# Two transfer cuts in a decode attention + gated MLP kernel: w_up in three transfers, the last wo tile in fewer pieces

## The chip, the core and the metric

The kernel runs on one core of a Trainium2 chip. The metric is the time of one execution in microseconds (us). A core has a matmul engine (PE, with a separate weight-load path, PEld), a vector engine (DVE), a scalar engine (ACT), a general engine (POOL) and a queue engine (SP) that issues most transfers. The transfers themselves are carried by 16 DMA engines, which is what "load engines" means in this text. A transfer is cut into packets, here one packet for one partition's row, and every DMA engine works its packets off in order; after its share of a transfer it sends a small packet of 4 bytes that counts up the transfer's semaphore. A transfer has landed when all its engines have done so.

## What is computed

One decode step for two sequences: y = x + attention(xn) @ wo + (relu(xn @ w_gate) * (xn @ w_up)) @ w_down, where xn is x normalized over its 512 columns. Attention has 32 query heads of 128 over 8 key heads, and looks at the last 4,096 positions of the caches.

```python
q = (xn @ wq) as 32 heads of 128
k, v = the last 4096 positions of k_cache, v_cache (8 heads, each used by 4 query heads)
o = softmax(q k^T / sqrt(128)) v
a = o (2 x 4096) @ wo (4096 x 512)
gate = xn @ W_gate (512 x 1792); gate = gate * (gate > 0)
h = gate * (xn @ W_up)
out = x + a + h @ W_down (1792 x 512)
```

All of it is fp32. The weights and the part of the caches that is used are 94.9 MB, and each byte is read once.

## The kernel before

All loads but x go out from SP, in the order in which the program is written: wq in two transfers, w_gate, w_up, then k and v tiles of 4 MB in turn, w_down, and wo in two tiles. Each of these lands in a tile of a ring of four buffers (tag "ring", 28 or 32 KB in each of the 128 partitions), so that a load can be issued when the tile four places before it has been used. Before the change every load spans 128 partitions; x alone has two rows and goes to partitions 0 and 1.

The middle of the program is a loop over four groups of heads: for each k tile two 32x32 block transposes on DVE (line L253), score matmuls on PE (L258), a softmax, a re-ordering of the weights on DVE (L302), and the matmuls with v (L321).

Names and lines that matter here:

- `load_ff` loads w_gate (tile wg) and w_up (tile wu): 128 partitions with 4 rows of 1,792 floats each, 28 KB in a partition. The matmuls that read them are on L229; first the 16 of w_gate, then the 16 of w_up (u_ps). Their product (L238, L239) is wanted only by the w_down matmuls near the end.
- The last wo tile (r = 1) holds 16 "rows" j of 128 x 512 floats, 2 KB of each partition for one row. It comes in pieces, `cuts` on line L441: rows 0 to 3, 4 to 7, 8 to 11, 12 and 13, 14, each piece with a transfer and a semaphore of its own; row 15 (`last`) follows in two halves of its columns (L449).
- The matmuls at the end take the rows in order. Rows 0 to 7 go the wide way (`project_wide`, L424, tile yw_ps), together with all of the first wo tile; ACT then copies the sum to SBUF (yw, L454). Rows 8 to 14 go the narrow way (`project`, L428, tile y_ps): four matmuls a row, each in two passes. After row 11 the same function folds yw into y_ps. DVE copies y_ps out (yc, L460) when row 14 is in. Row 15 is multiplied last, half by half (z_ps, L464), DVE adds yc to it (yo, L467), and SP sends the result (L469).

The order on each engine is the order of the program text; there is no scheduler. Completion semaphores of the loads are dealt out in turn from a set of eight, so that a load also waits until the load eight places before it has landed.

Of the kernel before, what the change touches and what calls it, by code (L numbers as in the profile page):

```python
# [9 lines left out]
F32 = mybir.dt.float32  # L10
# [10 lines left out]
def kernel(  # L21
# [12 lines left out]
    nc = tc.nc  # L34
    P = 128
# [4 lines left out]
    F = w_gate.shape[1]  # L40
    W = min(4096, max(256, SK // 4))
    KC = D // P
# [17 lines left out]
    ring = ctx.enter_context(tc.tile_pool(name="ring", bufs=RING))  # L60
# [8 lines left out]
    def load(name, src, shape):  # L69
        t = ring.tile(shape, F32, name=name, tag="ring")  # L70
        nc.sync.dma_start(t, src)
        return t
# [5 lines left out]

    def load_ff(w, name):
        return load(name, w.rearrange("(p k) f -> p k f", p=P), [P, KC, F])  # L80

    def load_down():
        return load("wd", w_down.rearrange("(p k) e -> p k e", p=P), [P, FB, D])
# [11 lines left out]
    NJ = HQ * DH // (R * P)  # L95
# [3 lines left out]
    def wo_rows(r, j0, j1):  # L99
        rows = NJ * P  # L100
        return wo[r * rows:(r + 1) * rows, :].rearrange("(p j) e -> p j e", p=P)[:, j0:j1, :]
# [93 lines left out]
    for kc in range(KC):  # L195
        for r in range(R):
            for c in range(C):
# [3 lines left out]
                    start=(kc == 0), stop=(kc == KC - 1),  # L201
                )
    gw = load_ff(w_gate, "wg")
    uw = load_ff(w_up, "wu")
    for r in range(R):
        qs = work.tile([P, 512], F32, name=f"qs{r}", tag="qs")
        (nc.vector.tensor_copy if r else nc.scalar.copy)(qs, q_ps[r])  # L207
# [5 lines left out]
        for m in range(NB):  # L213
            src = qt[32 * m:32 * m + 32, :, :, 0].rearrange("p i (t h) b -> p b t h i", h=2)
            for x in range(Q):
                d = qz[32 * x:32 * x + 32, r * B:r * B + B, m]
                dst = bass.AP(
                    tensor=d.tensor, offset=d.offset + x * TK,
                    ap=[d.ap[0], d.ap[1], [64 + REP, NP], [32, 2], [1, REP]],
# [218 lines left out]
        project_wide(hT[:, k, 0:B], dw[:, k])  # L438
    spread_heads(R - 1)
    wots = []  # L440
    for r, cuts in ((0, (0, NJ)), (1, (0, 4, 8, 12, 14, 15))):  # L441
        wt = ring.tile([P, NJ, D], F32, name=f"wo{r}", tag="ring")
        for j0, j1 in zip(cuts, cuts[1:]):
            nc.sync.dma_start(wt[:, j0:j1], wo_rows(r, j0, j1))
        wots.append(wt)
# [54 lines left out]
```

## Time and profile before

| | |
|---|---|
| median of 3 runs | 228.81 us (228.78 to 228.83) |
| the profiled execution's own time | 228.73 us |
| its span, first to last instruction | 226.9 us |
| granted PE clock, mean | 0.804 |
| busy: PE / DVE / ACT / POOL | 127.3 / 118.6 / 14.1 / 4.3 us |
| bytes moved | 95.03 MB, mean 419 GB/s |

The profiled execution lies 0.08 us under the median of the runs and 0.05 us under the fastest of them. The span leaves out 1.8 us of the execution's own time, which lie before the first and after the last instruction.

How to read it: the profile gives the busy time of each engine, the share of time in which the 16 DMA engines had a packet, and a chain of waits that ends with the last instruction. The view of a stretch of time (a window) gives the same for a part of the span, and the view of the DMA queues for a window gives the number of packets that began in it, their bytes, and the time they took as a share of 16 engines over the window's length. From such a row the mean duration of a packet is share x window x 16 / packets. Queue q1 is SP's, q10 is ACT's (x), q8 carries the instruction fetches.

### The profile page before, as it was taken

How to read it: one execution, taken by the hardware profiler on the slowest of the kernel's cores; microseconds unless marked ns; L12 is line 12 of the kernel's file. 1: busy time of each engine (PE TensorE's matmuls, PEld its weight loads, DVE VectorE, ACT ScalarE, POOL GpSimd, SP SyncE). 2: the span in 40 equal slices, each digit the busy share in tenths (PEclk: the TensorE clock that was granted, in tenths of full speed). 3: DMA queues.
4: the chain of work that ended last, by engine and by line, in shares of the span. 5: the costliest groups of instructions: out<-in, count | busy, mean ns of one | idle time of the engine just before them, and what ended most of it. 6: DMA issues, size and time to landing. Idle time of an engine off the chain costs nothing.

```text
span 226.9 us, 2121 instructions
## 1 busy us (share of the span) xinstructions
PE 127.3 (56%) x888; PEld 37.2 (16%) x888; DVE 118.6 (52%) x159; ACT 14.1 (6%) x41; POOL 4.3 (2%) x15
## 2 busy tenths in 40 slices
PE   0195926502735004885705885936957646869294
PEld 0141211100101001221201211201411201214013
DVE  2400043219893399964599993599369285130001
ACT  2000123000000500000200000200000110000000
POOL 7000000000000000000000000000000000000000
PEclk9999788955796555796985996585997995999589
DMA  7999999998998998998999999999999899999892
GB/s 278 462 393 427 475 414 413 462 445 387 462 456 375 458 456 387 448 462 387 445 462 422 407 462 433 404 456 442 399 450 456 387 448 462 409 423 459 377 414 85
DMA packets 4212, 95.03 MB, mean 419 GB/s; under 512 B 488, under 2 KB 748, under 8 KB 1004
## 3 DMA queue, kind: packets, MB, share of 16 engines
q1 hardware_dynamic: 4196, 94.90, 97.4%
q8 instruction: 7, 0.11, 0.2%
q14 instruction: 1, 0.01, 0.0%
q10 hardware_dynamic: 8, 0.00, 0.0%
HBM read 94.90 MB, written 0.00 MB: 418 GB/s over the span
## 4 chain that ended last, share of the span: by engine, by line
DMA 58%; DVE 23%; PE 12%; issue 3%; ACT 2%; SPq 1%; DVEq 0%; ACTq 0%
DMA k<-in_A_k_cache_dram 38%; DVE kT L253 16%; DMA wo<-in_A_wo_dram 11%; DMA wq<-in_A_wq_dram 9%; DVE pt L302 4%; PE o L321 3%; PE s L258 3%; PE q_ps L199 2%; ACT pz L290 1%; DVE on L330 1%; DVE pT L296 1%; PE y_ps L428 1%; PE oa L341 1%; DVE m L270 1%; ACT L290 1%
## 5 line engine op out<-in xcount | busy, mean ns | idle before, releaser
L253 DVE STREAM_TRANSPOSE kT<-k 128x4096 f32<-128x4096 f32 x16 | 70.6, 4429 | 11.9 <-DMA k<-in_A_k_cache_dram 11.8
L258 PE MATMUL s<-kT,qz 128*32 128x512 f32 x256 | 43.3, 800 | 56.7 <-DVE kT L253 56.7
L321 PE MATMUL o<-v,pt 128*32 128x512 f32 x256 | 33.5, 655 | 0.0
L258 PEld LDWEIGHTS s<-kT,qz 128*32 128x32 f32 x256 | 8.5, 126 | 85.1 <-issue 59.8
L302 DVE COPY pt<-pT 32x256 f32<-32x256 f32 x64 | 18.2, 284 | 1.0
L341 PE MATMUL oa<-on,pick 128*16 128x512 f32 x16 | 10.0, 712 | 6.9 <-DVE on L330 6.9
L221 DVE COPY qz<-qt 32x32 f32<-32x32 f32 x16 | 3.0, 188 | 20.3 <-ACT qz L221 20.3
L199 PE MATMUL q_ps<-wq,xnT 128*32 128x512 f32 x64 | 11.8, 901 | 3.1 <-DMA wq<-in_A_wq_dram 2.7
L321 PEld LDWEIGHTS o<-v,pt 128*32 128x32 f32 x256 | 9.0, 119 | 19.0 <-issue 18.9
L290 ACT ACTIVATE pz<-s,nm 64x512 f32<-64x512 f32 x8 | 5.8, 729 | 80.4 <-DVE nm L284 80.3
L330 DVE TENSOR_TENSOR on<-o,own_u 128x512 f32<-128x512 f32 x8 | 5.4, 672 | 9.9 <-PE o L321 9.8
L460 DVE COPY yc<-y_ps 128x128 f32<-128x128 f32 x1 | 0.3, 292 | 19.4 <-PE y_ps L428 19.4
L296 DVE STREAM_TRANSPOSE pT<-pz 128x1024 f32<-128x1024 f32 x4 | 5.0, 1245 | 8.3 <-ACT pz L290 8.3
L424 PE MATMUL yw_ps<-wo,oT 128*2 128x512 f32 x48 | 6.8, 724 | 4.2 <-DMA wo<-in_A_wo_dram 4.2
L270 DVE TENSOR_REDUCE m<-s 128x1 f32<-128x512 f32 x4 | 2.8, 692 | 11.5 <-PE s L258 11.5
L184 PE MATMUL xt_ps<-rep,xc 2*128 2x32 f32 x8 | 2.1, 419 | 10.7 <-DVE rep L182 10.7
L229 PE MATMUL u_ps<-wu,xnT 128*32 128x448 f32 x32 | 3.2, 542 | 2.8 <-DMA wu<-in_B_W_up_dram 2.8
L199 PEld LDWEIGHTS q_ps<-wq,xnT 128*32 128x32 f32 x64 | 2.5, 155 | 11.5 <-issue 7.2
L229 PE MATMUL g_ps<-wg,xnT 128*32 128x448 f32 x32 | 4.4, 704 | 0.0
L424 PE MATMUL yw_ps<-wd,hT 128*2 128x512 f32 x28 | 3.6, 592 | 1.1 <-DMA wd<-in_B_W_down_dram 1.1
L210 PE MATMUL qt<-ident,qs 128*128 128x128 f32 x8 | 1.7, 353 | 4.4 <-DVE qs L207 4.4
L359 PEld LDWEIGHTS op<-osb,spread 16*128 16x128 f32 x32 | 3.7, 187 | 1.8 <-issue 1.8
(73 smaller groups left out, 54.4 us busy)
## 6 DMA issues: line engine op xcount, KB each, us to landing
k<-in_A_k_cache_dram SPq DMA_DIRECT2D x8, 4096.0 KB, 24.3
v<-in_A_v_cache_dram SPq DMA_DIRECT2D x8, 4096.0 KB, 27.0
wq<-in_A_wq_dram SPq DMA_DIRECT2D x2, 4096.0 KB, 16.6
wo<-in_A_wo_dram SPq DMA_DIRECT2D x1, 4096.0 KB
wg<-in_B_W_gate_dram SPq DMA_DIRECT2D x1, 3584.0 KB, 29.2
wu<-in_B_W_up_dram SPq DMA_DIRECT2D x1, 3584.0 KB, 38.6
wd<-in_B_W_down_dram SPq DMA_DIRECT2D x1, 3584.0 KB, 28.1
wo<-in_A_wo_dram SPq DMA_DIRECT2D x3, 1024.0 KB, 22.4
```

Of the source, the lines that this page charges most:

```text
L199: nc.tensor.matmul(q_ps[r][32 * c:32 * c + 32, :], xnT[:, kc, :], wqt[kc // 2][:, kc % 2, n * 512:(n + 1) * 512], start=(kc == 0), stop=(k ...
L229: nc.tensor.matmul(dst[32 * c:32 * c + 32, :], xnT[:, kc, :], wt[:, kc, c * FQ:(c + 1) * FQ], start=(kc == 0), stop=(kc == KC - 1),)
L253: nc.vector.transpose(kt.rearrange("p j m i -> p j (m i)"), src)
L258: nc.tensor.matmul(ss[g][32 * q:32 * q + 32, :], qz[:, g, 2 * mh + m, a, h], kt[:, JS * s1:JS * s1 + JS, m, h::2], start=(a == 0 and mh == ...
L270: nc.vector.tensor_reduce(out=m, in_=ss[g], op=ALU.max, axis=AX.X)
L290: nc.scalar.activation(pv[o, :, :, h], ss[g][o].rearrange("p (j i) -> p j i", j=JS), AF.Exp, bias=nm[o], scale=SCALE, accum_out=l[o],)
L296: nc.vector.transpose(pT.rearrange("p j x t k -> p (j x t k)"), pz.rearrange("p j s -> p (j s)"))
L302: nc.vector.tensor_copy(pts[g][32 * x:32 * x + 32, :, s1, :, h], pT[q:q + 32, :, x].rearrange("p j t k -> p t j k"))
L321: nc.tensor.matmul(o[32 * q:32 * q + 32, :], pts[g][:, a, s1, j:j + 4].rearrange("p u h k -> p (u h k)"), v[:, lo:lo + 512], start=(s1 == ...
L330: nc.vector.tensor_tensor(ons[a], o.rearrange("p (u d) -> p u d", u=4), own_u[:, :, None].to_broadcast([P, 4, P]), op=ALU.mult)
L341: nc.tensor.matmul(oa[g].rearrange("h u d -> h (u d)"), pick[:, 8 - 8 * a:24 - 8 * a], ons[a].rearrange("p u d -> p (u d)"), start=(a == 0 ...
L424: nc.tensor.matmul(yw_ps[32 * c:32 * c + B, :], lhsT, w, start=(n < Q), stop=(n >= wide - Q))
```

## The change

w_up comes in three transfers in place of one. The first takes the whole 28 KB of partitions 0 to 111. The second takes the first 22 KB of partitions 112 to 127, so one partition's row for each of 16 DMA engines. The third takes the last 6 KB of those 16 partitions; its source is written as 4 x 4 rows, so that it is spread over four DMA engines, the lowest-numbered, with four rows each. Together a DMA engine of the four carries 7 x 28 + 22 + 4 x 6 = 242 KB of w_up, and one of the other twelve 7 x 28 + 22 = 218 KB; before, each carried 8 x 28 = 224 KB.

Rows 0 to 14 of the last wo tile come in three pieces, rows 0 to 7, 8 to 12, and 13 and 14, in place of five. Row 15 comes in two halves as before.

```diff
+    def load_up():
+        t = ring.tile([P, KC, F], F32, name="wu", tag="ring")
+        flat = t.rearrange("p k f -> p (k f)")
+        row, part, most = KC * F, 1536, P - 16
+        cut = row - part
+
+        def src(p0, ap):
+            return bass.AP(tensor=w_up.tensor, offset=w_up.offset + p0, ap=ap)
+
+        nc.sync.dma_start(flat[0:most], src(0, [[row, most], [1, row]]))
+        nc.sync.dma_start(flat[most:P, 0:cut], src(most * row, [[row, 16], [1, cut]]))
+        nc.sync.dma_start(flat[most:P, cut:row], src(most * row + cut, [[4 * row, 4], [row, 4], [1, part]]))
+        return t
...
-    uw = load_ff(w_up, "wu")
+    uw = load_up()
...
-    for r, cuts in ((0, (0, NJ)), (1, (0, 4, 8, 12, 14, 15))):
+    for r, cuts in ((0, (0, NJ)), (1, (0, 8, 13, 15))):
```

On SP, at the start of the program, the loads stand in this order before (a row is the line, the tile written and what it is read from, and partitions x floats):

```order
L71 DMA wg<-in_B_W_gate_dram 128x7168
L71 DMA wu<-in_B_W_up_dram 128x7168
L71 DMA k_0_266<-in_A_k_cache_dram 128x1x8192
```

and in the changed program:

```order
L71 DMA wg<-in_B_W_gate_dram 128x7168
L91 DMA wu<-in_B_W_up_dram 112x7168
L92 DMA wu<-in_B_W_up_dram 16x5632
L93 DMA wu<-in_B_W_up_dram 16x1536
L71 DMA k_0_268<-in_A_k_cache_dram 128x1x8192
```

Two loads are added ahead of the first k tile; nothing else on SP changes its place up to the last wo tile.

On PE, at the end of the program, the narrow matmuls stand like this before; DMAHW with a number is the semaphore of a load, Pool and Activation are semaphores of those engines:

```order
L428 MATMUL y_ps<-wo_840,oT_rows 32x128 [waits DMAHW2_49,Pool_49]
L428 MATMUL y_ps<-wo_840,oT_rows 32x128 x15
L428 MATMUL y_ps<-yw,fold_rows 32x128 [waits Activation_49]
L428 MATMUL y_ps<-yw,fold_rows 32x128 x3
L428 MATMUL y_ps<-wo_840,oT_rows 32x128 [waits DMAHW3_49]
L428 MATMUL y_ps<-wo_840,oT_rows 32x128 x7
L428 MATMUL y_ps<-wo_840,oT_rows 32x128 [waits DMAHW4_49]
L428 MATMUL y_ps<-wo_840,oT_rows 32x128 x3
```

and in the changed program:

```order
L442 MATMUL y_ps<-wo_842,oT_rows 32x128 [waits DMAHW3_49,Pool_49]
L442 MATMUL y_ps<-wo_842,oT_rows 32x128 x15
L442 MATMUL y_ps<-yw,fold_rows 32x128 [waits Activation_49]
L442 MATMUL y_ps<-yw,fold_rows 32x128 x3
L442 MATMUL y_ps<-wo_842,oT_rows 32x128 x4
L442 MATMUL y_ps<-wo_842,oT_rows 32x128 [waits DMAHW4_49]
L442 MATMUL y_ps<-wo_842,oT_rows 32x128 x7
```

The matmuls and their order are the same. The first wait now covers rows 8 to 12, and the second covers rows 13 and 14 together; the wait for row 14 alone is gone.

## The prediction

> **What bounds the kernel now.** I read the page first, then windows, then the end of the chain. The window rows give PE, PEld, DVE, ACT and POOL busy, the granted PE clock, the share of time in which the 16 DMA engines had a packet, and GB/s.
>
> ```profile
> span 226.9 us, 2121 instructions
> DMA 58%; DVE 23%; PE 12%; issue 3%; ACT 2%; SPq 1%; DVEq 0%; ACTq 0%
> ...
> 2.20:222.00 219.80, 125.30 (x833) 35.96 (x837) 117.94 (x156) 13.53 (x41) 2.66 (x9) 0.80 1.00 429
> 222.00:222.30 0.30, 0.30 (x20) 0.30 (x15) 0.00 (x0) 0.00 (x0) 0.00 (x0) 1.00 0.45 171
> 222.30:222.90 0.60, 0.60 (x28) 0.42 (x20) 0.00 (x0) 0.00 (x0) 0.00 (x0) 1.00 0.54 189
> 222.90:223.40 0.50, 0.48 (x16) 0.16 (x8) 0.00 (x0) 0.00 (x0) 0.00 (x0) 1.00 0.35 121
> 223.40:223.80 0.40, 0.40 (x20) 0.22 (x16) 0.20 (x1) 0.00 (x0) 0.00 (x0) 1.00 0.00 0
> ```
>
> From 2.2 to 222.0 us the DMA engines are busy all the time (1.00). The chain names other engines for 42% of the span, but there the next loads are under way anyway; whatever lengthens the load stream lengthens the kernel. At the end the engines do not stop together: by 222.0 us fewer than half have work (0.45 of 16 is 7), and these seven go on to 223.4. So seven DMA engines are some 1.4 us behind the other nine. Why is seen in the instruction fetches (all, and the one from 208 to 209 us) and in the price of a packet:
>
> ```profile
> q8 instruction: 7, 0.11, 0.2%
> ...
> q8 instruction: 1, 0.02, 5.5%
> ...
> q1 hardware_dynamic: 96, 3.15, 101.1%
> ...
> q1 hardware_dynamic: 104, 2.98, 98.6%
> ```
>
> The third row is the window from 99.0 to 106.2 us, with 32 KB packets alone: 1.011 x 7200 ns x 16 / 96 = 1213 ns each. The fourth is 23 to 30 us, 28 KB packets alone: 0.986 x 7000 x 16 / 104 = 1062 ns. The difference, 151 ns for 4 KB, makes **37.75 ns a KB**, and 5 ns are left for each packet. Seven instruction fetches of 16 KB fall on the load engines one by one; one takes 0.055 x 1000 x 16 = 880 ns, and an engine that is put back by it, with no idle time, never catches up.
>
> **The change part by part.** First the load stream of w_up, for one of the twelve upper engines: 218 KB in place of 224, so 6 x 37.75 = 226 ns less, with the same 8 packets. For one of the four lowest: 18 KB more, 680 ns, and 4 more packets, 20 ns: 700 ns. If these four are among the nine that are early, 0.70 is less than their lead of 1.4 us, and the last loads land 0.23 us earlier. Two more issues on SP cost about a microsecond there, and are hidden:
>
> ```profile
> wu<-in_B_W_up_dram SPq DMA_DIRECT2D x1, 3584.0 KB, 38.6
> v<-in_A_v_cache_dram SPq DMA_DIRECT2D x8, 4096.0 KB, 27.0
> 50.47 8.77 DVE L253 STREAM_TRANSPOSE kT<-k 128x4096 f32<-128x4096 f32 x2 [4.76 <-DMA k<-in_A_k_cache_dram]
> ```
>
> A 4 MB load takes an engine 8 x 1213 ns, 9.7 us, but lands 27.0 us after its issue: 17 us of loads are always queued ahead. PE waits for all of w_up once (it lands 38.6 us after its issue), but the vector work behind it is done 4.76 us before the first k tile lets DVE go on. Without that cover each 0.1 us there would be 0.1 us of kernel. The semaphores of the loads, eight in turn, shift by two and back again, since two loads are added and two taken away; only the second half of row 15 changes what it waits for on SP,
>
> ```profile
> SPq L449 <- DMA wd<-in_B_W_down_dram: 5.5, 1, 5.5
> ```
>
> and that wait goes. It is worth nothing: up to 222.0 us no DMA engine stands idle that an earlier issue could fill.
>
> That leaves the second transfer: 16 DMA engines, each with one 22 KB row, into 16 neighbouring partitions. At the usual price a row takes 22 x 37.75 + 5 = 836 ns. But no load of this trace on q1 writes fewer than 128 partitions, so nothing shows that sixteen engines write sixteen neighbours at full rate. The only load with fewer is x: two rows, partitions 0 and 1, in two halves of 1 KB a row. These are the rows of q10 in windows of 15, 25, 30 and 30 ns in which one such packet begins each; q1 is a packet of wq that begins in the last of them:
>
> ```profile
> q10 hardware_dynamic: 1, 0.00, 18.3%
> ...
> q10 hardware_dynamic: 1, 0.00, 21.5%
> ...
> q10 hardware_dynamic: 1, 0.00, 9.6%
> ...
> q1 hardware_dynamic: 1, 0.03, 252.7%
> q10 hardware_dynamic: 1, 0.00, 9.6%
> ```
>
> In the first half the two packets overlap, so two engines carry them (they begin in 1.650 to 1.665 and in 1.665 to 1.690 us): one takes 0.183 x 15 x 16 = 44 ns, the other 0.215 x 25 x 16 = 86 ns, twice as much. In the second half (6.05 and 6.08 us) both take 0.096 x 30 x 16 = 46 ns, one right behind the other, and a 32 KB packet beside them 2.527 x 30 x 16 = 1213 ns, as ever. So two writers of neighbouring partitions took turns when they met on idle engines; but 1 KB squeezed in beside running streams cost nobody anything that can be seen. The first speaks for a path into memory that several partitions share and that carries one engine's rate; the second, that a little can be absorbed.
>
> If they take turns, how many share a path? Sixteen engines keep their full rate into 128 partitions, so there are at least 16 paths, 8 partitions each; sixteen neighbours then lie on as few as two paths (eight writers each) or, with two on one path as for x, on as many as eight. A row of 22 KB then takes between 2 and 8 times its 831 ns of data: 0.83 to 5.8 us more, on all sixteen engines, with nothing to hide it. I take the middle by ratio, four writers on a path: 3 x 831 = **2.49 us**. Below lies nothing (no turns); a gain is excluded, since the bytes are the same. Above lies more, if the 7 rows that each engine has of the 112 partitions also meet others: all of the 7 doubled would be 7 x 1.06 = 7.4 us. Shares of 7 rows no longer match paths of 8 partitions, but only a part of the rows would meet; I allow half, 3.7 us, as the upper end.
>
> [...]
>
> Then the end. The chain and the timeline from 220.8 us (start, duration, engine, line):
>
> ```profile
> 196.85 24.33 DMA wo<-in_A_wo_dram
> 221.19 0.14 issue
> ...
> 220.80 0.58 ACT L454 COPY yw<-yw_ps 128x512 f32<-128x512 f32 x1 [10.73 <-PE yw_ps L424]
> 221.32 1.08 PE L428 MATMUL y_ps<-wo,oT_rows 128*32 128x128 f32 x32 [0.60 <-DMA wo<-in_A_wo_dram]
> 222.19 0.43 PE L428 MATMUL y_ps<-yw,fold_rows 128*32 128x128 f32 x8
> 222.45 1.09 PE L428 MATMUL y_ps<-wo,oT_rows 128*32 128x128 f32 x24
> 223.11 0.16 PEld L428 LDWEIGHTS y_ps<-wo,oT_rows 128*32 128x32 f32 x8 [0.29 <-DMA wo<-in_A_wo_dram]
> 223.44 0.16 PEld L464 LDWEIGHTS z_ps<-wo,oT_rows 128*32 128x32 f32 x8 [0.18 <-DMA wo<-in_A_wo_dram]
> 223.60 0.29 DVE L460 COPY yc<-y_ps 128x128 f32<-128x128 f32 x1 [19.39 <-PE y_ps L428]
> 224.00 0.35 DVE L467 TENSOR_TENSOR yo<-z_ps,yc 128x64 f32<-128x64 f32 x2
> 224.38 0.69 SPq L469 DMA_DIRECT2D out_dram<-yo  x1
> ```
>
> Rows 8 to 11 land at 221.19 and start at 221.32; four rows take until 222.19, so 0.2175 us a row, and the fold has as many passes as a row. Row 14 starts at 223.11 when it lands, and 0.49 later yc starts. Now count the new pieces. Two transfers and 16 packets fewer save about 16 x 5 + 10 = 90 ns of the stream. But rows 8 to 12 land as one: 16 KB more to wait for, 604 ns, less the 8 packets and a semaphore saved by then, 49 ns: 0.555 later than rows 8 to 11 did. With w_up's 0.23 earlier, they start at 221.32 + 0.555 - 0.226 = 221.65. From there PE has rows 8 to 11 (0.87), the fold (0.22), rows 12 and 13 (0.435), and 0.49 for row 14: yc at 223.66 where it was 223.60. Rows 13 and 14 land long before their turn, and row 15 at about 223.4, also before. So the merged pieces turn a gain of 0.31 us of the stream (0.226 + 0.09) into **0.06 us lost**: the last wait is now rows 8 to 12, no longer row 14.
>
> The sum: 2.49 + 0.06 = +2.55 us. The profiled execution took 228.73, 0.08 less than the median 228.81; against the median this gives 231.36, so **231.4 us**.
>
> **The rivals.** (1) **No turns.** The second transfer runs at the usual 836 ns. For it: the 46 ns packets, and 1.00 busy whatever engine lags whichever. Against it: 44 and 86. Then +0.06: 228.9 us, no change; the balance works and the end eats it. If my end is wrong by the whole 0.37 (0.31 + 0.06) it is 228.5, still within 0.2%. (2) **The lowest four are behind, not ahead.** No row numbers the DMA engines; seven of sixteen are behind. Without turns the latest would then end 0.70 - 0.09 = 0.61 us later; the last half of row 15, and all behind it, by as much: 229.4 us. (3) **Turns in larger groups, and in the first transfer too**: 228.8 + 0.06 + 5.8 = 234.7 us, or 2.55 + 3.7 = 6.25 more, 235.1.
>
> **How the numbers follow.** About 0.2% (0.46 us) is what a measurement of this kernel can tell from no change. Turns among two to six or so (my forecast, 230 to 233 us): 0.40. Rival 3: 0.13. Rival 1: 0.38. Rival 2: 0.05. The rest, 0.04, is a gain over 0.46 us by something I do not see: the pieces that I can add up give 0.31 at most. Slower is 0.40 + 0.13 + 0.05 = 0.58, same 0.38, faster 0.04. Forecast and rival 1 are nearly level; the 86 ns of x tip it. The range has to hold rival 1 and the turns: 228.4 to 234.8. The forecast's own range is 229.7 (pairs, 228.81 + 0.06 + 0.83) to 234.7.
>
> **What would show it.** Right: in the profile of the changed kernel the DMA share stays at 1.00 but GB/s falls for two or three microseconds around 39 us, the packets of 22 KB take some 3.3 us in place of 0.84, the first k tile reaches DVE at about 53 us, and every load after it is as late. Wrong: 22 KB packets of 836 ns, and k at 50.2. For the end: PE should start rows 8 to 12 without a gap before row 13, and yc should follow row 14 with no wait for a load; if a wait for rows 13 and 14 shows, the end is mis-sized. A shorter stretch with only some engines at work at the end would show the balance. I am wrong altogether if the upper twelve gain more than 0.31 us.

## The result, and the profile after

The changed kernel takes **237.01 us** (median of 5 runs, 236.80 to 237.05) where the kernel before takes 228.83 (5 runs, 228.78 to 228.94): 1.0352 times as long, 95% interval 1.0341 to 1.0363; the medians are 8.2 us apart. The prediction was 231.4 with a range up to 234.8. The sign was right, the size was not.

From the page of the changed kernel, the rows that answer to those of before: the span, the data rate in 40 slices of 5.88 us, the packets of all queues, and the shares of the chain that ended last.

```profile
span 235.1 us, 2123 instructions
GB/s 274 441 446 424 468 239 305 166 425 418 424 435 440 446 442 424 421 418 435 440 446 440 415 429 418 438 440 446 435 424 429 413 438 446 415 460 421 415 401 68
DMA packets 3972, 95.03 MB, mean 404 GB/s; under 512 B 488, under 2 KB 748, under 8 KB 892
DMA 59%; DVE 20%; PE 14%; issue 3%; ACT 2%; SPq 0%; DVEq 0%; ACTq 0%
```

The span is 8.2 us longer too (226.9 before), the bytes are the same, and the kernel is still bound by its load stream. The windows of the changed kernel (busy time of PE, PEld, DVE, ACT and POOL, the clock, the DMA share, GB/s) say where it went:

```profile
2.20:30.00 27.80, 14.95 (x76) 5.04 (x76) 4.11 (x16) 1.77 (x5) 2.66 (x9) 0.88 0.97 417
30.00:40.00 10.00, 5.95 (x36) 1.95 (x36) 3.51 (x16) 2.73 (x16) 0.00 (x0) 0.66 1.04 283
40.00:52.00 12.00, 3.90 (x24) 1.33 (x28) 0.62 (x1) 0.30 (x1) 0.00 (x0) 0.72 1.02 287
52.00:60.00 8.00, 1.16 (x16) 0.14 (x4) 3.77 (x3) 0.00 (x0) 0.00 (x0) 0.71 0.98 422
60.00:200.00 140.00, 78.58 (x502) 21.20 (x502) 102.69 (x114) 7.92 (x18) 0.00 (x0) 0.78 1.00 432
```

Read the last two columns together. The DMA share stays at 1.0 throughout, but from 30 us, where the first transfer of w_up begins, the data rate falls to two thirds, and by the slices of the page (239, 305 and 166, from 29.4 to 47.0 us) it is back at about 47. The engines count as busy although their packets take longer. The prediction looked for two or three such microseconds around 39 us; there are some seventeen, and they begin with the **first** transfer. How long a packet of that transfer takes can be read from a window in which SP's queue carries nothing else (31 to 39 us; queue, packets, MB, share of 16 engines):

```profile
q1 hardware_dynamic: 78, 2.24, 103.7%
```

1.037 x 8000 ns x 16 / 78 = 1702 ns for 28 KB that took 1062 before. Seven such rows for each engine are 7 x 640 = 4.5 us lost. For the second transfer the window from 42.00 to 42.10 us has two rows of 22 KB and two signals (the small packets with which an engine reports its end), for the third the window from 44.05 to 44.13 us two rows of 6 KB and two signals:

```profile
q1 hardware_dynamic: 4, 0.05, 275.7%
...
q1 hardware_dynamic: 4, 0.01, 146.6%
```

2.757 x 100 x 16 = 4411 ns, where 2 x (836 + 9) = 1690 would be usual, and 1.466 x 80 x 16 = 1876 ns, where 2 x (231 + 9) = 480 would be. So the rows of all three transfers are slow. Windows with one packet each give the means: 2308 ns for the sixteen rows of 22 KB, not the 3.3 us that the prediction looked for, and 814 ns for the sixteen of 6 KB. From the timeline of the changed kernel (start, duration):

```profile
57.79 8.77 DVE L267 STREAM_TRANSPOSE kT<-k 128x4096 f32<-128x4096 f32 x2 [2.97 <-DMA k<-in_A_k_cache_dram]
...
229.19 0.58 ACT L468 COPY yw<-yw_ps 128x512 f32<-128x512 f32 x1 [11.31 <-PE yw_ps L438]
229.72 1.08 PE L442 MATMUL y_ps<-wo,oT_rows 128*32 128x128 f32 x32 [0.60 <-DMA wo<-in_A_wo_dram]
230.59 0.43 PE L442 MATMUL y_ps<-yw,fold_rows 128*32 128x128 f32 x8
230.81 0.86 PE L442 MATMUL y_ps<-wo,oT_rows 128*32 128x128 f32 x24
231.46 0.43 PE L478 MATMUL z_ps<-wo,oT_rows 128*32 128x64 f32 x16
231.73 0.29 DVE L474 COPY yc<-y_ps 128x128 f32<-128x128 f32 x1 [18.80 <-PE y_ps L442]
232.13 0.36 DVE L481 TENSOR_TENSOR yo<-z_ps,yc 128x64 f32<-128x64 f32 x2
232.51 0.69 SPq L483 DMA_DIRECT2D out_dram<-yo  x1
```

The first k tile reaches DVE at 57.79 in place of 50.47, 7.32 us later (the prediction had about 53); yc starts at 231.73 in place of 223.60, 8.13 later. So nine tenths are there when w_up is in, and 0.8 us come after it. The end itself ran as foreseen: rows 8 to 12 in one piece, then the fold, then rows 12 to 14 without a wait for a load; yc 2.01 us after the first narrow matmul, as the sum had it (223.66 - 221.65).

One more thing stands in the packet count. Before, the page has 4212 packets. Two wo transfers less are 2 x (128 + 16) = 288 fewer. w_up has 144 data packets in place of 128, 16 more. That makes 3940, and the page has 3972: 32 more, which are the 4-byte packets with which each engine of a transfer signals its end, 16 for each of the two added transfers. **The third transfer went over all 16 engines, not over four** (four would have signalled 4 times: 3960). Under 512 B the page has 488 packets, as before: 32 fewer and 32 more.

### The profile page after: what moved, and what is told of

The parts are those of the page before. It is cut to its first block, busy times and chain, and to the rows that moved or that the text cites. A ratio compares the mean times of both kernels' runs of the same rounds, so it can differ in the third digit from the quotient of the medians.

```text
span 235.1 us, 2123 instructions
## 1 busy us (share of the span) xinstructions
PE 129.8 (55%) x888; PEld 38.1 (16%) x888; DVE 118.8 (51%) x159; ACT 14.2 (6%) x41; POOL 4.3 (2%) x15
## 2 busy tenths in 40 slices
DMA packets 3972, 95.03 MB, mean 404 GB/s; under 512 B 488, under 2 KB 748, under 8 KB 892
## 4 chain that ended last, share of the span: by engine, by line
DMA 59%; DVE 20%; PE 14%; issue 3%; ACT 2%; SPq 0%; DVEq 0%; ACTq 0%
DMA k<-in_A_k_cache_dram 40%; DVE kT L267 13%; DMA wo<-in_A_wo_dram 10%; DMA wq<-in_A_wq_dram 9%; PE s L272 4%; DVE pt L316 4%; PE o L335 3%; PE q_ps L213 3%; PE oa L355 2%; ACT pz L304 1%; DVE pT L310 1%; PE y_ps L442 1%; DVE on L344 1%; DVE m L284 1%; ACT L304 1%
## 5 line engine op out<-in xcount | busy, mean ns | idle before, releaser
L272 PE MATMUL s<-kT,qz 128*32 128x512 f32 x256 | 45.1, 829 | 56.9 <-DVE kT L267 56.9
L335 PE MATMUL o<-v,pt 128*32 128x512 f32 x256 | 30.9, 611 | 0.0
L272 PEld LDWEIGHTS s<-kT,qz 128*32 128x32 f32 x256 | 9.4, 133 | 86.2 <-issue 62.0
L355 PE MATMUL oa<-on,pick 128*16 128x512 f32 x16 | 11.7, 825 | 6.9 <-DVE on L344 6.9
L213 PE MATMUL q_ps<-wq,xnT 128*32 128x512 f32 x64 | 12.3, 940 | 3.6 <-DMA wq<-in_A_wq_dram 3.3
L335 PEld LDWEIGHTS o<-v,pt 128*32 128x32 f32 x256 | 8.5, 112 | 17.2 <-issue 17.1
L243 PE MATMUL u_ps<-wu,xnT 128*32 128x448 f32 x32 | 5.1, 799 | 8.5 <-DMA wu<-in_B_W_up_dram 8.5
L438 PE MATMUL yw_ps<-wo,oT 128*2 128x512 f32 x48 | 7.4, 784 | 4.2 <-DMA wo<-in_A_wo_dram 4.2
L252 DVE TENSOR_TENSOR hh<-gs,u_ps 128x448 f32<-128x448 f32 x1 | 0.6, 621 | 12.3 <-PE u_ps L243 12.3
L355 PEld LDWEIGHTS oa<-on,pick 128*16 128x16 f32 x16 | 1.6, 115 | 15.0 <-DVE on L344 9.6
```

The lines of the kernel that those rows point to most:

```text
L213: nc.tensor.matmul(q_ps[r][32 * c:32 * c + 32, :], xnT[:, kc, :], wqt[kc // 2][:, kc % 2, n * 512:(n + 1) * 512], start=(kc == 0), stop=(k ...
L243: nc.tensor.matmul(dst[32 * c:32 * c + 32, :], xnT[:, kc, :], wt[:, kc, c * FQ:(c + 1) * FQ], start=(kc == 0), stop=(kc == KC - 1),)
L272: nc.tensor.matmul(ss[g][32 * q:32 * q + 32, :], qz[:, g, 2 * mh + m, a, h], kt[:, JS * s1:JS * s1 + JS, m, h::2], start=(a == 0 and mh == ...
L335: nc.tensor.matmul(o[32 * q:32 * q + 32, :], pts[g][:, a, s1, j:j + 4].rearrange("p u h k -> p (u h k)"), v[:, lo:lo + 512], start=(s1 == ...
L355: nc.tensor.matmul(oa[g].rearrange("h u d -> h (u d)"), pick[:, 8 - 8 * a:24 - 8 * a], ons[a].rearrange("p u d -> p (u d)"), start=(a == 0 ...
L438: nc.tensor.matmul(yw_ps[32 * c:32 * c + B, :], lhsT, w, start=(n < Q), stop=(n >= wide - Q))
```

## The experiments

All were compared with the kernel before, run on the same chip. Brackets behind "times" hold the 95% interval, and a difference in us is worked out from that ratio. In the code cuts, <...> stands for a source that is not written out.

**The two parts of the change apart, and w_up cut in two other ways.** The first has the new pieces of the last wo tile alone:

```
-    for r, cuts in ((0, (0, NJ)), (1, (0, 4, 8, 12, 14, 15))):
+    for r, cuts in ((0, (0, NJ)), (1, (0, 8, 13, 15))):
```

> The kernel before with the new pieces of the last wo tile alone (rows 0 to 7, 8 to 12, 13 and 14, 15), w_up as before. My theory of the end, from the rows of before: rows 8 to 12 land 0.555 us later than rows 8 to 11 did and nothing shifts them forward now, so PE starts them at 221.88 in place of 221.32 and yc starts at 221.88 + 0.87 + 0.22 + 0.435 + 0.49 = 223.89 in place of 223.60: +0.29 us, 229.1. The load stream itself ends 0.09 us earlier. Rival: the merged pieces carry a good part of the 8.2 us that were lost; then 231 us or more.

Measured: 229.25 us, 1.0016 times (1.0007 to 1.0024), +0.37 us (0.16 to 0.55). The end is what the prediction worked out. The second has the three transfers of w_up alone:

```
-    uw = load_ff(w_up, "wu")
+    uw = load_up()          # as in the change
```

> The three transfers of w_up alone, the last wo tile in its five old cuts. If all but the 0.3 us of the end comes from w_up: the changed kernel's 237.0 less 0.3, so 236.7 us, and the first k tile reaches DVE at about 57.8 us as in the changed kernel. If the two parts cost only together: under 231 us.

Measured: 237.59 us, 1.0375 times (1.0344 to 1.0405). w_up carries the loss. That this is 0.6 above the changed kernel, though the 0.37 of the end is not in it, lies within its scatter (237.03 to 238.61): the loss itself varies by more than the end is worth. The third leaves the rows whole, so that no transfer is meant for four engines:

```
+        nc.sync.dma_start(flat[0:most], src(0, [[row, most], [1, row]]))
+        nc.sync.dma_start(flat[most:P], src(most * row, [[row, 16], [1, row]]))
```

> w_up in two transfers of whole rows: 112 partitions x 28 KB (7 rows for each engine) and 16 partitions x 28 KB (one row for each engine). Nothing goes over four engines alone, so each of the 16 has the same 8 rows as before. Theory A, turns in the 16 neighbouring partitions alone: the last row takes 2 to 4 times its 1.06 us, +1.1 to +3.2 us, 229.9 to 232.0. Theory B, the rows of the 112 partitions collide too: by what the changed kernel shows between 30 and 52 us, +6 to +8 us, 235 to 237. Theory C, the transfer over four engines carries the loss: 228.8 to 229.0.

Measured: 237.01 us, 1.0348 times (1.0334 to 1.0362): theory B, and the same time as the changed kernel. Theories A (229.9 to 232.0) and C are out. The fourth cuts w_up in three by columns, each over all 128 partitions:

```
+        for c0, c1 in ((0, cut), (cut, cut + 1024), (cut + 1024, row)):
+            nc.sync.dma_start(flat[:, c0:c1], src(c0, [[row, P], [1, c1 - c0]]))
```

> w_up in three transfers as in the change, but each over all 128 partitions (22, 4 and 2 KB of every row), so each engine has the same bytes and the same set of partitions as before. If the partitions reached are what costs: only 16 more packets at 5 ns for each engine and two more issues, +0.1 us, 228.9. If cutting w_up in three, the smaller packets or the order of the queue is what costs: some microseconds, up to 236.

Measured: 229.08 us, 1.0011 times (1.0002 to 1.0020), +0.25 us (0.05 to 0.46). Its windows at the place where the changed kernel falls to 283 and 287 GB/s:

```profile
30.00:40.00 10.00, 6.25 (x48) 2.21 (x52) 3.58 (x14) 2.48 (x12) 0.00 (x0) 0.83 1.00 424
40.00:52.00 12.00, 2.21 (x24) 0.52 (x16) 3.08 (x3) 0.00 (x0) 0.00 (x0) 0.74 1.00 432
```

Three transfers are harmless; which partitions a transfer reaches is not.

**The price of the partitions, measured by itself.** For these the kernel before stays whole, and one load that nobody reads goes behind w_up, into a ring tile of its own. All four take that tile, so whatever the tile itself costs is in the load over 128 partitions too. They differ in one line:

```
     uw = load_ff(w_up, "wu")
+    extra = ring.tile([P, KC * F], F32, name="extra", tag="ring")
+    row = KC * F
+    nc.sync.dma_start(extra[P - 16:P, 0:5632], <16 rows of 22 KB>)     # 112 to 127
or   nc.sync.dma_start(extra[0:P:8, 0:5632], <the same>)                # every eighth
or   nc.sync.dma_start(extra[:, 0:704], <128 rows of 2.75 KB>)          # all, the same bytes
or   nc.sync.dma_start(extra[0:112], <112 rows of 28 KB>)
```

> The kernel before and, right behind w_up, one more load that nobody reads: 22 KB into each of the 16 neighbouring partitions 112 to 127, one row for each of the 16 engines. No turns: one packet of 836 ns on every engine, +0.84 us. Turns of two: +1.7. Turns of four (the term of my prediction, 4 x 0.831): +3.3. Turns of eight: +6.6.

> The same extra load (16 rows of 22 KB, one for each engine, nobody reads it), into partitions 0, 8, 16 up to 120. If a path serves 8 neighbouring partitions, each engine has a path of its own: +0.84 us. [...] If only the few partitions of a transfer count, wherever they lie: as much as for 16 neighbours.

> As many extra bytes (352 KB, nobody reads them) over all 128 partitions, 2.75 KB of each: the measure for the other two. At 37.75 ns a KB and 5 ns a packet, 8 packets for each engine: +0.87 us.

> The kernel before and one more load that nobody reads: 28 KB into each of the partitions 0 to 111, 7 rows for each engine. If 7 rows for each engine cost what 8 do: 7 x 1.062 = +7.4 us. If the rows of the 112 partitions collide, as between 30 and 52 us of the changed kernel: half of them twice as long +11.1, all of them +14.9.

| extra load | us | times before (95%) | more, us | its own packets, us |
|---|---|---|---|---|
| 16 neighbours, 22 KB | 233.27 | 1.0193 (1.0172 to 1.0214) | 4.4 | 0.84 |
| every eighth, 22 KB | 231.51 | 1.0118 (1.0103 to 1.0133) | 2.7 | 0.84 |
| all 128, 2.75 KB | 229.75 | 1.0036 (1.0022 to 1.0050) | 0.8 | 0.87 |
| 112, 28 KB | 243.42 | 1.0619 (1.0566 to 1.0671) | 14.2 | 7.4 |

The load over all 128 partitions costs its packets and nothing else, so an extra load is a fair measure. The 16 neighbours cost 3.6 us beyond their packets, more than turns of four (2.49) and less than turns of eight (5.8). The 112 partitions cost 6.7 us beyond theirs (5.5 to 7.9). Every eighth partition cost 2.7 us where its packets are 0.84, so paths do not serve eight neighbours each. In the profile with the 16 neighbours, the window from 38.62 to 39.07 us has their rows:

```profile
DMA packets 30, 0.34 MB, mean 751 GB/s; under 512 B 15, under 2 KB 15, under 8 KB 15
q1 hardware_dynamic: 30, 0.34, 440.5%
```

Fifteen of the 30 are signals of 9 ns; 4.405 x 450 ns x 16 less these, over 15 rows, is 2105 ns for 22 KB in place of 836. That is 1.3 us more, and the load costs 3.6: the rest falls on packets behind it, 32 KB into their usual partitions (a row of these stands in the last section).

**Same stride, same bytes, other place.** The sharpest pair: 16 rows of 22 KB into every fourth partition, from 32 to 92 or from 0 to 60.

```
+    nc.sync.dma_start(extra[32:96:4, 0:5632], <the same 16 rows>)
or   nc.sync.dma_start(extra[0:64:4, 0:5632], <the same 16 rows>)
```

> The extra load again (16 rows of 22 KB, one for each engine, nobody reads it), into every fourth partition from 32 to 92. If neighbours by eights share a path, two writers meet on each of 8 paths: +1.7 us or, at the surcharge that the 16 neighbours showed (4.4 where 3.3 was worked out), +2.2. If it counts only how few partitions a transfer has, or how large its packets are: +2.7 or more, as for every eighth partition. [...]

> The same, into every fourth partition from 0 to 60: the stride, the bytes and the packets are those of its twin from 32 to 92, only the start is another. If the place in the memory does not matter beyond distance: the same time as its twin. [...]

Measured: from 32, 229.78 us, 1.0040 times (1.0026 to 1.0054), **+0.9**, under both theories; from 0, 230.98 us, 1.0092 times (1.0077 to 1.0107), **+2.1**. From the profile of the first, 38.71 to 38.90 us:

```profile
DMA packets 18, 0.20 MB, mean 1067 GB/s; under 512 B 9, under 2 KB 9, under 8 KB 9
q1 hardware_dynamic: 18, 0.20, 250.2%
```

2.502 x 190 ns x 16, less nine signals of 9 ns, is 836 ns for each of the nine rows: not one of them meets another. Same stride and packets, and no loss in one place, 1.2 us in the other. So the place decides; no row shows which partitions share a path, if any do. Over the four places of sixteen rows 0.9, 2.1, 2.7 and 4.4 us were measured, for packets of 0.84. Rows of 836 ns that take equal turns would make, by estimate, 1.7 us in twos, 3.3 in fours and 6.6 in eights: the 0.9 are the packets alone, 2.1 and 2.7 lie between twos and fours, 4.4 between fours and eights.

**Several rows for each engine.** The same pair with 64 partitions of 28 KB, four rows for each engine:

```
+    nc.sync.dma_start(extra[0:64], <64 rows of 28 KB>)
or   nc.sync.dma_start(extra[32:96], <the same>)
```

> An extra load that nobody reads, 28 KB into each of partitions 0 to 63, four rows for each engine. Its own packets: 4 x 1.062 = +4.25 us. [...]

> The twin: 28 KB into each of partitions 32 to 95, four rows for each engine. If a transfer of fewer than 128 partitions is slow as such: as much as partitions 0 to 63. [...]

Measured: 0 to 63, 239.91 us, 1.0479 times (1.0464 to 1.0495), **+11.0**; 32 to 95, 233.17 us, 1.0186 times (1.0169 to 1.0203), **+4.26**, which is the packets' own 4.25. Sixty-four partitions are as good as 128 in one place and cost 2.6 times as much in the other. From the two profiles, 0 to 63 in the window from 41 to 45 us:

```profile
DMA packets 24, 0.66 MB, mean 165 GB/s; under 512 B 1, under 2 KB 1, under 8 KB 1
q1 hardware_dynamic: 24, 0.66, 80.9%
```

and 32 to 95 in the window from 39.4 to 42.3 us:

```profile
DMA packets 48, 1.35 MB, mean 465 GB/s; under 512 B 1, under 2 KB 1, under 8 KB 1
q1 hardware_dynamic: 48, 1.35, 107.6%
```

0.809 x 4000 x 16 / 23 = 2251 ns a row, against 1.076 x 2900 x 16 / 47 = 1062: 2.12 times as long, a little worse than two engines taking turns. The turns are argued from the time, since no row names a path. Four such rows are 9.0 us; the load costs 11.0 in all, where equal turns in twos would make 2 x 4.25 = 8.5. Where the other 2.0 fall is not shown.

**The transfer that was meant for four engines.** As the change writes it (4 x 4 rows of 6 KB), as an extra load into partitions 112 to 127 and into 0 to 15:

```
+    nc.sync.dma_start(extra[P - 16:P, 0:1536], <[4 * row, 4], [row, 4], [1, 1536]>)
or   nc.sync.dma_start(extra[0:16, 0:1536], <the same>)
```

> The kernel before and, behind w_up, one extra load that nobody reads, made as the third transfer of the change: 6 KB into each of partitions 112 to 127, four rows for each of four engines, 0.93 us of packets for each of these. If the four have a lead that hides it and no path is shared: 0.0 us. If the owners of those partitions are pushed back by the 96 KB that come over their paths: +0.9 (each path carries 24 KB more) to +1.8 (turns).

> The same extra load over four engines, into partitions 0 to 15. If it is the four engines' own time that counts: as much as its twin in 112 to 127. If paths count, and the four lowest engines are those that bring partitions 0 to 15 in an ordinary load, no other engine is touched and only the four are 0.93 us later: hidden by their lead, 0.0 to 0.3 us, and at least 0.6 us less than its twin.

Measured: 229.99 us, 1.0048 times (1.0033 to 1.0063), +1.1; and 229.74 us, 1.0039 times (1.0026 to 1.0052), +0.9. Both theories of each expected four engines; there were sixteen. From the second profile, 38.50 to 39.02 us:

```profile
DMA packets 38, 0.22 MB, mean 429 GB/s; under 512 B 19, under 2 KB 19, under 8 KB 34
```

34 less 19 are 15 packets of 6 KB that begin within 0.52 us. At 6 x 37.75 + 5 = 231 ns each, four engines could begin at most twelve. The rows themselves are not slow here. The window from 38.860 to 38.896 us has three of them with their signals, the one from 39.04 to 39.16 us the first 32 KB packets of k on eight engines, with eight signals:

```profile
q1 hardware_dynamic: 6, 0.02, 126.6%
...
q1 hardware_dynamic: 16, 0.26, 708.5%
```

1.266 x 36 x 16 less 27, over 3, is 234 ns for a row, the usual price; 7.085 x 120 x 16 less 72, over 8, is 1691 ns for a 32 KB packet in place of 1213. The 0.9 us is near 4 x 0.23, what turns of four would give, but what goes beyond the load's own 0.23 falls on the packets behind it. Then the same rows as four transfers of four:

```
+    for i in range(4):
+        nc.sync.dma_start(extra[0 + i:16:4, 0:1536], <4 rows of 6 KB, 4 * row apart>)
or   nc.sync.dma_start(extra[112 + i:128:4, 0:1536], <the same>)
```

> The extra load of 6 KB into each of partitions 0 to 15 that nobody reads, now as four transfers of four rows each (partitions 0, 4, 8, 12; then 1, 5, 9, 13; and so on), so that it can only go over four engines, four packets for each. The profile should show 4 x 4 data packets and 4 x 4 semaphore packets more, and the engines that land first no later than before. If the four lowest engines have a lead of 1.4 us: their 0.93 us are hidden, 0.0 to 0.3 us. If they have none: +0.9.

> The same four transfers into partitions 112 to 127, as the change wanted its third transfer. The four engines have the same work as in the twin. If a path into the memory carries one engine's rate however many engines write on it, the four paths of these partitions get 24 KB more, 0.93 us, and their owners are late by that: +0.9 to +1.8 us. If only the engines' own time counts: as the twin.

Into 0 to 15: 229.34 us, 1.0028 times (1.0019 to 1.0037), +0.6 (the medians are 0.43 apart). In a window as long, 38.79 to 39.31 us, its profile has

```profile
DMA packets 27, 0.22 MB, mean 422 GB/s; under 512 B 13, under 2 KB 13, under 8 KB 22
```

nine packets of 6 KB, which four engines can do; and its page counts 4244 packets, 32 more than before, so 16 rows and 16 signals, four signals for each of the four transfers. In this profile the first k tile is no later than before (50.25 us in place of 50.47), so there the 0.93 us of these four engines seem to be hidden by a lead; where the 0.6 us come from is not shown. Into 112 to 127 the runs lay between 230.30 and 251.38 us (four runs), too uneven for a comparison; the only profile is that of the 230.3. It was never faster than its twin, and why it is so uneven stays open. Last, the change's w_up with a third part that truly goes over four engines, the last wo tile in its old pieces:

```
-        nc.sync.dma_start(flat[most:P, cut:row], src(most * row + cut, [[4 * row, 4], [row, 4], [1, part]]))
+        for i in range(4):
+            nc.sync.dma_start(flat[most + i:P:4, cut:row], src((most + i) * row + cut, [[4 * row, 4], [1, part]]))
```

> The change's w_up with its third part truly over four engines (four transfers of four rows of 6 KB), the last wo tile in its old cuts. If the loss is in the transfers of 112 and 16 partitions, as the 22 KB and 28 KB rows of e3_112_16 say: 235 to 239 us, no better than the three transfers alone (237.6), and perhaps as uneven from run to run as d4r_up. If the loss came from the third part not going over four engines: the balance works now, and the time falls by 0.9 us or more, below 236.5.

Measured: 237.55 us, 1.0374 times (1.0353 to 1.0395). The change as it was described would have lost as much.

**Does it add up elsewhere?** w_up in three transfers of whole rows, one of them in the good place:

```
+        for p0, p1 in ((32, 96), (0, 32), (96, 128)):
+            nc.sync.dma_start(flat[p0:p1], <p1 - p0 rows of 28 KB>)
```

> w_up in three transfers of whole rows: partitions 32 to 95, then 0 to 31, then 96 to 127. The 64 cost nothing beyond their bytes if paths decide (d64_32). In each of the two others two engines meet on each of eight paths, two rows for each engine, so four rows in all, as in d64_0, where four such rows cost 11.0 us in place of 4.25: +6.75 us, 235.6. Without the surcharge, each path at one engine's rate: +4.25, 233.1. If a transfer of fewer than 128 partitions were slow as such, the 64 would add to it: over 238.

Measured: 234.05 us, 1.0220 times (1.0201 to 1.0238), **+5.0** (4.6 to 5.5): between the 4.25 of plain turns and the 6.75 taken from the 64 partitions. Both take it that two engines meet on each path in the two sets of 32 as well; that is an estimate carried over from partitions 0 to 63, and no run shows it. Its first transfer, 31 to 34 us,

```profile
DMA packets 48, 1.38 MB, mean 459 GB/s; under 512 B 0, under 2 KB 0, under 8 KB 0
q1 hardware_dynamic: 48, 1.38, 106.2%
```

runs at 1.062 x 3000 x 16 / 48 = 1062 ns a row. The place decides here too; what a place costs beyond turns is not one factor.

## Why the prediction was right in sign and wrong in size

**The bound was right.** All that w_up lost reached the end (7.3 us at the first k tile, 8.1 at yc), and 0.87 us of extra packets over 128 partitions moved the time by 0.8.

**The first transfer is the term that failed.** The sum had nothing for it: its 112 rows were taken at the usual 1062 ns. Half of its rows doubled, 3.7 us, stood only as an upper end and in rival 3. Measured were 7 x 640 ns = 4.5 us in the changed kernel, and 6.7 beyond its packets for the same 112 partitions as an extra load (4.9 in its profiled run, the fastest of the four at 241.17 us). The text even had a reason for it, seven rows for each engine against paths of eight partitions, and put it aside as an upper end. If the rows go to the engines seven in a row, an engine writes partitions that another engine has in an ordinary load, and does so from the first row on; that assignment is argued, no row of a trace names it.

**The second transfer's term came near in size.** By itself, as an extra load, the transfer loses 3.6 us, where 2.49 was worked out. In the changed kernel its sixteen rows take 2308 ns on average in place of 836, so 1.47 us, and the 32 KB packets of k behind all three transfers lose 1.35 us more: at most 2.8 us together. Four writers on a path, the middle by ratio, was the author's estimate, and the expectations that count four paths for sixteen neighbours rest on it too; no run shows the number. Equal turns of four would be 3.3 us for every row; the rows took 2105 ns as an extra load and 2308 in the changed kernel.

**The third transfer was misread.** The prediction took the words of the change for what the program does: 226 ns less for twelve engines and 700 ns more for four. It went over sixteen engines, one row for each (no row numbers them, so nothing shows a lowest four either), into the same 16 partitions, and its rows took 814 ns on average in place of 231, 0.58 us more; as an extra load it costs 1.1 us, 0.9 beyond its 0.23. How much of this it adds by itself is not separated: the two transfers of 112 and 16 whole rows, with the same bytes in the same partitions, took the same 237.01 us. "The change does not do what it says" was not among the rivals. That the four rows times four, evenly spaced, are taken as one list of sixteen is the likely reason, an inference: written as four lists of four they went over four engines, with four signals for each list.

**The accounts.** In the profile of the changed kernel, packet by packet from 30 to 60 us, the time beyond the usual price, summed over the 16 engines and divided by 16, is 4.54 us for the 112 rows of the first transfer, 1.47 for the 22 KB rows, 0.58 for the 6 KB rows and 1.35 for the 32 KB packets of k behind them: 7.9 us, against 7.3 at the first k tile and 8.1 at yc. So more than half of the loss is the term that the sum left out. Measured as extra loads the three would come to 6.7 + 3.6 + 0.9 = 11.2 us; why they cost less in a row is not shown.

**The end was right.** Without the gain from w_up its sum is +0.29 us, +0.37 (0.16 to 0.55) was measured alone, and the profile has no wait for rows 13 and 14. The gain of 0.226 that was to pay for it did not exist, since nothing was balanced. Of the 0.8 us between the first k tile and yc that leaves 0.4, which is within the scatter: in the profiles of the other runs with the old end, the stretch from the first k tile to yc lasts between 173.0 and 173.9 us (173.1 before, 173.9 in the changed kernel).

**The evidence for turns was not evidence.** The 86 ns of x tipped the forecast. In the profile with the one extra load of 6 KB rows into 0 to 15, windows of 6 and 19 ns (1.655 to 1.661 and 1.661 to 1.680 us) in which the two packets begin have

```profile
q10 hardware_dynamic: 1, 0.00, 53.1%
q10 hardware_dynamic: 1, 0.00, 14.5%
```

51 and 44 ns, fully overlapped and neither doubled; with the load into 112 to 127 one of them (1.645 to 1.652 us) has

```profile
q10 hardware_dynamic: 1, 0.00, 362.5%
```

3.625 x 7 x 16 = 406 ns. The durations of so small a packet at the start scatter; one of them says nothing about paths. That the rows would be slowed held (2308 ns in place of 836); its ground did not.

Of the rivals, no turns (228.9) is refuted by rows of 22 KB that took 2105 ns as an extra load and 2308 in the changed kernel, the lowest four behind (229.4) fell with the transfer that it was about, and rival 3 (234.7 or 235.1) named the right place with a chance of 0.13. With the first transfer's 3.7 in the sum the forecast would have been 235.1.

## What to carry to other kernels

A load that reaches fewer than all 128 partitions can have a price that its bytes do not show: 64 partitions of 28 KB cost 4.26 us in one place and 11.0 in another. Cut a large load by columns, which cost 0.25 us here, and if it must be cut by partitions, measure each transfer of the cut as an extra load in its own place, and not only the smallest. Count a transfer's packets and signals on the page before believing how many engines carry it.

## What the runs showed that was not expected

A DMA share of 1.00 is no sign of a full data rate: between 30 and 52 us of the changed kernel it stays at 1.02 to 1.04 while the rate is 283 to 287 GB/s. And the excess shows up in the wrong packets: 22 KB rows of 2105 ns are followed by 32 KB packets into ordinary partitions that are slow as well. From the profile with the extra load into the 16 neighbours, 43.1 to 43.6 us:

```profile
q1 hardware_dynamic: 13, 0.43, 234.8%
```

2.348 x 500 x 16 / 13 = 1445 ns in place of 1213, four to five microseconds after those rows began. In the profile with the 6 KB rows into 0 to 15 it was all there, 1691 ns against rows of 234. The packet that is slow is thus not always the one that is in the wrong place; the stretch has to be read as a whole.
